# A fused convolution and SwiGLU kernel: the value half takes its feature chunks in turned order, fetches go to 128 partitions, and one queue carries all transfers

## The chip, the cores and the metric

The kernel runs on one core of a Trainium2 chip. The metric is the device time of one execution in microseconds. A profiled execution gives the span from the first to the last instruction of the program and the trace that the lines below come from.

## The reference

Two blocks follow each other. The first is a causal depthwise convolution with 7 taps, softmaxed per head (8 heads of 24 channels), over x of 8 x 4096 x 192. The second is a SwiGLU layer without bias over the resulting 32768 tokens.

```python
w = softmax(weight)                       # 8 heads x 7 taps
x = conv(x_padded, w)                     # (8, 4096, 192) -> (32768, 192)
rms = np.sqrt(np.mean(x * x, axis=-1, keepdims=True) + 1e-06)
xn = x / rms * rms_g
g = xn @ w_gate                           # 192 -> 1536
silu = g * (1.0 / (1.0 + np.exp(-g)))
val = xn @ w_val                          # 192 -> 1536
return (silu * val @ w_out).astype(np.float32)   # 1536 -> 192
```

## The kernel before

**Tiling.** The tokens are taken in 32 "pairs" of 1024 (two groups g of T = 512). The 192 features are three chunks of 64 rows (`KP = 3`, `HP = 64`). Partitions 0 to 63 (`LOW`) compute the gate product and partitions 64 to 127 (`UPP`) the value product, side by side on TensorE; each half needs all three chunks of the tokens, so the normalized tokens stand twice in SBUF, in three slots (k = 0, 1, 2) of the tile `xb` (`rb`). In the kernel before, slot k has chunk k in both halves.

**The way of one pair.** Two pairs ahead of its products, x is loaded to `xh` (L148, eight transfers `ld`, one for each head, runs of 96 bytes; nine in every fourth pair), convolved (`cv`, L442), squared and summed, and scaled by POOL (`mul`, L492). Eight transfers `pl` (`put_away`, L1050) write the heads to a tile `xd` in DRAM, features by tokens. The transfers `ft` (`fetch`, L638) bring `xd` back into `xb`. Then each slot is split in three parts: ACT copies a rounded part (`n`, L667), DVE makes two more (`l` L816, `d` L818); sums of slots 0 and 1 (`x_sum`, L833) are split in the same way. TensorE multiplies the parts with weight pieces (L906), ACT takes silu (L983), DVE multiplies with the value product (L990), and TensorE makes the output product (L933). Transfers `st` (`leave`, L1039) write the result.

**The ring.** The split weights lie in DRAM (`wd`, written by `prepare`, L768). Each pair needs 45 pieces of 192 KB, through a ring of 10 slots in SBUF. `ring_load` (L785) is put on SyncE's queue at the place of the last product that uses a slot, and waits there for TensorE.

**What sets the order.** The order of all work is written out by hand in strings: `FIRST` for the first pair, then `ORDER` for each pair, and `LINE` for TensorE's products. The letter ahead of a word is its engine: A is ACT, V DVE, G POOL, S SyncE; `p3` means three products. Instructions of one engine, transfers included, run in that order, so a transfer that waits holds up what stands behind it on its queue. Hardware semaphores of transfers go round eight lanes over both queues: a transfer waits until the one eight places before it has landed. `queue(eng)` picks ACT's queue for A and SyncE's for S. In the steady part ACT issues the eight `pl`, both halves of slot 0 (`ft.0`, `ft.1`) and five of the ten `st`; SyncE issues the ring loads, `ft.2` to `ft.5`, the `ld` and the other five `st`.

**Pieces in xb.** A row of 1024 tokens is kept as `CUT = 4` pieces of 256, each followed by two unused elements (`GAP = 258`), so that one row of a fetch is four runs of 1 KB. `lent` (in the space of the later ring) has the same form for pair 2.

**Pair 0** has no fetch: `cross` turns it on TensorE and copies it to `xb` in a layout of its own, where the value half already has other chunks than the gate half; `AT` (L1071) says which weight slot belongs to which.

Of the kernel before, what the change touches and what calls it, by code (L numbers as in the profile page):

```python
# [11 lines left out]
F32 = mybir.dt.float32  # L12
F32R = mybir.dt.float32r
AF = mybir.ActivationFunctionType
ALU = mybir.AluOpType
# [5 lines left out]
def kernel(  # L21
# [10 lines left out]
    nc = tc.nc  # L32
    P = nc.NUM_PARTITIONS
# [10 lines left out]
    T = 512  # L44
    PT = 2 * T
    NJ = PT // P
    HALO = K - 1
    HP = P // 2
    KP = D // HP
# [9 lines left out]
    LOW, UPP = slice(0, HP), slice(HP, P)  # L59
# [5 lines left out]


    NP = FC // 2
    CUT = 4
    GAP = PT // CUT + 2
    SPAN = 1509  # L70
    SPLIT = 2.0**-12
    HIGH = 0xFFFFF000
# [2 lines left out]
    ORDER = (  # L75
        "Vd.0 An.4 An.3 Ac2- p5- Gh4.2- Vl.2 Vd.4 Vh4.3- Vl.3 Vd.3 Vl.0 Vd.2 Vh4.0- Vh4.5-",
        "p8- Gh4.4- Gh4.1- VT11- VC22- p2- p1 Gl.4 Acv0+ Af1.0 VT22- VC21- p1- VT21- p3 Vcv1+",
        "p1 Af3.0 Ast1.2- Vcv2+ Vf4.0 p3- p3 Aga.0 Ast1.0- Vcv3+ VT12- Vma.0 Sst0.2- Agc.0",
        "Ast0.3- p1 Vf5.0 p2 Vcv4+ p1 Vmc.0 Vcv5+ p2 Sst1.3- p1 Sst0.4- Sst0.0- Agb.0 Ast1.1-",
        "Agc.1 Ast0.1- Vmb.0 p2 Vcv6+ Agd.0 p2 Aga.1 Vmd.0 Vma.1 Vmc.1 p1 Asq+ Vred+ p1 Af1.2",  # L80
        "Sst1.4- Gh1.0 Agb.1 Vmb.1 p1 Gpow+ p3 Af3.2 p1 Vf4.2 p4 Aga.2 Agd.1 Vma.2 Vbc+ Vf5.2",
        "Gmul+ p1 Agc.2 p1 Apl.0+ Apl.1+ Apl.2+ p1 Vmd.1 Vmc.2 p6 Agd.2 Agb.2 Apl.3+ Vmb.2",
        "Vmd.2 Apl.4+ p1 Agb.3 Aga.3 Apl.5+ p1 Vmb.3 Vma.3 p4 Af1.4 Vf3.4 Agc.3 Apl.6+ Apl.7+",
        "p3 Vmc.3 p1 Vf4.4 p2 Aga.4 Gh1.1 p1 Agd.3 Aft.0+ Sft.2+ Vma.4 Vf5.4 Vh3.1 Sft.3+",
        "Aft.1+ Sld.0++ Vmd.3 Sft.4+ Sld.1++ Sft.5+ Sld.2++ Sld.3++ Sld.4++ Sld.5++ Sld.6++",
        "Sld.7++ p7 Gh1.3 Agc.4 Agd.4 Vmc.4 Vmd.4 Agb.4 p1 Vh1.2 Vh3.0 Vmb.4 p7 An.0+ p1",
        "Aga.5 Agd.5 p1 Vh1.4 An.1+ Vx1+ Vmd.5 Vma.5 p1 Gh3.3 p2 Gh3.2 Agb.5 p2 Gh3.4 p2 Gx3+",
        "Agc.5 Vd.1+ p1 Vh2.0 Vmc.5 Vh2.1 Vmb.5 Vh1.5 Vh2.2 Vh3.5 Vl.1+ Vh2.5 Vh2.4 Ac1 p1",
# [2 lines left out]
    FIRST = (  # L91
        "p1 Vcv5+ W p2 Vcv6+ p1 Aga.0 Vma.0 p2 Asq+ W W p1 Agb.0 W Vmb.0 W p1 Vred+ p2 Agc.0",
        "Vmc.0 W p1 Gpow+ W W W p1 W p1 Agd.0 W Vmd.0 p1 Vbc+ Vh1.0 p1 Gmul+ p1 Aga.1 Vh3.0 W",
        "Vma.1 p1 W W W W p1 W p1 Agb.1 Apl.0+ Vmb.1 p1 Apl.1+ p1 Apl.2+ W p1 Agc.1 Apl.3+ W",
        "W W Vmc.1 Apl.4+ p1 W W Apl.5+ p1 Apl.6+ p1 Agd.1 Apl.7+ Vmd.1 p1 Vh1.1 W p1 W W W",
        "p1 Aga.2 Vh3.1 W Vma.2 W p3 Agb.2 Vmb.2 W p1 W W W p1 W p1 Agc.2 W Vmc.2 p3 Agd.2 W",
        "Vmd.2 p1 W W W Vh1.2 W p1 W p1 Aga.3 Vh3.2 Vma.3 p2 W p1 Agb.3 W W W Vmb.3 p1 W W p1",
        "Aft.0+ p1 Aft.1+ Agc.3 Sft.2+ Vmc.3 p1 Sft.3+ W p1 Sft.4+ W W W Sft.5+ p1 Agd.3 W",
        "Vmd.3 W p1 Vh1.3 p2 Aga.4 Vh3.3 Vma.4 W p1 W W p1 W p1 Agb.4 W Vmb.4 p3 Agc.4 W",
        "Vmc.4 p1 W p2 Agd.4 An.1+ Vmd.4 Sld.0++ p1 Vx1+ Vh1.4 p1 Gx3+ Vd.1+ p1 Aga.5 Vh3.4",  # L100
        "Sld.1++ Vma.5 Vl.1+ p1 Gx2+ p1 An.2+ p1 Agb.5 Gx4+ Vmb.5 p1 Sld.2++ p1 Sld.3++ p1",
        "Agc.5 Vmc.5 p1 Sld.4++ p1 Sld.5++ Agd.5 p1 An.0+ Vmd.5 p1 Sld.6++ Vh2.0 Vh1.5 p2",
        "Gh2.3 Sld.7++ Vh3.5 Vh2.5 p1 Vh2.1 p1 Vh2.4 p1 Ac1 Vh2.2 p2 R p7 As7 p7",
    )
    LINE = (
        "P1.0 P5.0 P6.0 P2.0 Q1.0 P7.0 P3.0 Q2.0 Ac.1 Q4.0 Q3.0 P4.0 Bc.1 Ec.1 Aa.1 Ba.1 Ea.1",
# [8 lines left out]
    cst = ctx.enter_context(tc.tile_pool(name="cst", bufs=1))  # L115
# [13 lines left out]
    def queue(eng):  # L129
        return nc.scalar if eng == "A" else nc.sync  # L130
# [31 lines left out]
    def load(p):  # L162
# [34 lines left out]
        out=ps[6][:, 0 : H * K], lhsT=ones[:], rhs=w_row[:], start=True, stop=True,  # L197
# [4 lines left out]
    rg_sb = cst.tile([P, KP], F32, name="rg_sb")  # L202
    rg = moe_rms_g.rearrange("(c p) -> p c", p=HP)
# [4 lines left out]
    spc = ctx.enter_context(tc.tile_pool(name="spc", bufs=1))  # L208
# [6 lines left out]
    def words(w):  # L215
        return w.bitcast(U32).rearrange("r (n two) -> r n two", two=2)
# [5 lines left out]
    def load_in(u, q):  # L222
        cols = slice(u * NF * P, (u + 1) * NF * P)
        t = big.tile([P, 2, NF, T], F32, name="ht")
        t = t[:].rearrange("p a f t -> p (a f t)")[:, 0 : KP * NF * P * 2].bitcast(U32)
        t = raw["in", u] = t.rearrange("p (k n two) -> p k n two", k=KP, two=2)
        if u == 0:
            hold(t[:, :, 0, 0].bitcast(F32))
        for w, rows in ((moe_w_gate, LOW), (moe_w_val, UPP)):
            for k in range(KP):  # L230
                q.dma_start(out=t[rows, k], in_=words(w)[k * HP : (k + 1) * HP, cols, :])  # L231

    few = 5
    big1 = spc.tile([P, 22, T], F32, name="part1")
    room1 = big1[:].rearrange("p i t -> p (i t)")
    lent = spc.tile([P, KP * CUT * GAP], F32, name="ring")
    early = room1[:, 10 * T + NJ * D : 10 * T + 4 * NJ * D].rearrange("p (i n) -> p i n", i=3)
    kept = [early[:, i].rearrange("p (j d) -> p j d", d=D) for i in range(3)]
    kept = itertools.cycle(kept)
# [5 lines left out]
    tt = work.tile([P, 9, T], F32, name="tt")  # L245
# [3 lines left out]
    def load_out(i):  # L249
# [22 lines left out]
        out=taps[:], in0=w_sb, in1=stat[:].to_broadcast([P, H, K]), op=ALU.subtract  # L272
# [68 lines left out]
        yield  # L341


    rb = cst.tile([P, KP * CUT * GAP], F32, name="xb")
    xb = rb[:, 0 : KP * PT].rearrange("p (k g t) -> p g k t", k=KP, g=2)

    def pieces_in(t):
        t = t[:, 0 : KP * CUT * GAP].rearrange("p (k c t) -> p k c t", k=KP, c=CUT)
        return t[:, :, :, 0 : PT // CUT]

    rb, lent4 = pieces_in(rb), pieces_in(lent)

    def tokens(p):
        return lent4 if p == 2 else rb
    spare = room1[:, 0 : 10 * T]

    def part(at, m, n):
# [276 lines left out]

    def fetch(p, i, eng="S"):

        k, rows = i // 2, (LOW, UPP)[i % 2]
        queue(eng).dma_start(  # L638
            out=tokens(p)[rows, k],
            in_=scr[p][k * HP : (k + 1) * HP, :].rearrange("p (c t) -> p c t", c=CUT),  # L640
        )

    free = [[0, 1, 2, 3], [0, 1, 2, 3]]

# [147 lines left out]
    def split_of(g, i):  # L792

        if not xsplit:
            xsplit.append(spc.tile([P, 8, T], F32, name="part0"))
            xsplit.append(spc.tile([P, 22, T], F32, name="part1"))
        t, at = ((0, 0), (1, 0), (1, 6), (1, 12), (1, 16))[g]
        if g == 4 and i == 0:
            t, at = 0, 6
        return xsplit[t][:, at + i * 2 : at + (i + 1) * 2, :]  # L800

    def cut(t):
        return t.rearrange("p g (c t) -> p (g c) t", t=PT // CUT)

    def operand(g, p):
        if g < KP:
            return tokens(p)[:, g]
        return cut(tt[:, 0:2, :] if g == 3 else tt[:, 2:4, :])

    def split(act, g, eng, p):  # L810
        src, high, low, mix = operand(g, p), *(cut(split_of(g, i)) for i in range(3))
        e = engine.get(eng)
        if act == "n":
            copy(eng, high.bitcast(F32R), src)
        elif act == "l":
            e.tensor_tensor(out=low.bitcast(F32R), in0=src, in1=high, op=ALU.subtract)  # L816
        else:
            nc.vector.scalar_tensor_tensor(  # L818
                out=mix.bitcast(F32R), in0=high, scalar=1.0 + SPLIT, in1=src,
                op0=ALU.mult, op1=ALU.subtract,  # L820
            )

    def x_sum(i, eng, p):
        n = CUT // 2
        a11, a21, a12, a22 = (
            tokens(p)[:, k // 2, k % 2 * n : (k % 2 + 1) * n] for k in range(4)
        )
        s1, s2, s4, s3 = (cut(tt[:, k : k + 1, :]) for k in range(4))
        dst, a, b, op = {
            1: (s1, a21, a22, ALU.add), 3: (s3, a11, a21, ALU.subtract),  # L830
            2: (s2, s1, a11, ALU.subtract), 4: (s4, a12, s2, ALU.subtract),
        }[i]
        engine[eng].tensor_tensor(out=dst, in0=a, in1=b, op=op)  # L833
# [3 lines left out]
    class Pair:  # L837
# [32 lines left out]
        def products(self):  # L870
            if self.p == 1:
                for j, c in PLAIN:
                    g, f = CELL[c]
                    self.open((j, c), False)
                    for k in range(KP):
                        for h in range(2):
                            nc.tensor.matmul(  # L877
                                out=self.both(j, c)[:, h, :], lhsT=wf[HALF[h], k, 2 * j + f, :],
                                rhs=rb[HALF[h], k, g * CUT // 2 : (g + 1) * CUT // 2],
                                start=(k == 0), stop=(k == KP - 1),  # L880
                                skip_group_check=True,
                            )
                        yield
                todo = [w for w in line_of if w[0][0] == "o"]
            else:
                todo = line_of
            for w, i in todo:
                if w[0] == "o":
                    self.step(int(w[1:]), int(i))
                else:  # L890
                    self.product(w, int(i))
                yield
# [175 lines left out]
        else:  # L1068
            {"sq": square, "red": reduce, "pow": factor, "bc": spread, "mul": scale}[act](p)

    AT = (0, 2, 1), (1, 2, 0)  # L1071

    def plain(hts):

# [107 lines left out]
    load_in(1, nc.sync)  # L1182
    conv_first((1, 3, 5, 6), 2)
    nc.sync.dma_start(out=rg_sb[LOW, :], in_=rg)
    nc.sync.dma_start(out=rg_sb[UPP, :], in_=rg)
    load(1)
    load_in(2, nc.sync)
    load_in(3, nc.sync)
# [99 lines left out]
```

## Time and profile before

| | us |
|---|---|
| median of 3 runs | 2496.06 |
| lowest, highest | 2494.13, 2496.62 |
| profiled execution, its own time | 2501.12 |
| its span | 2499.0 |
| granted TensorE clock | 1.00 of full speed |
| DMA, mean over the span | 165 GB/s |
| packets, share of 16 engines, SyncE's queue (q1) | 567088, 57.9% |
| packets, share of 16 engines, ACT's queue (q10) | 172226, 9.8% |

How to read it: PE is TensorE, PEld its weight loads, DVE VectorE, ACT ScalarE, POOL GpSimd, SP SyncE. Names such as "xb<-xd" give output and input by the program's tiles: "xb<-xd" is a fetch, "xd<-xh" a put, "ring<-wd" a ring load. "SPq" and "ACTq" are transfers issued, or waits, by the engine's sequencer. The chain of work that ended last is followed back from the last instruction through whatever released each step. In a list in order of time the columns are start and length in us, then engine, line and names; a bracket gives the engine's idle time just before and what ended it.

### The profile page before, as it was taken

To read this page: it belongs to the slowest core of one execution; us is meant where nothing else is said; L and a number is where in the kernel's file an instruction comes from. 1 tells how busy PE (TensorE), PEld (TensorE's weight loads), DVE (VectorE), ACT (ScalarE), POOL (GpSimd) and SP (SyncE) were. 2 spreads that over 40 slices of the span, in tenths; PEclk is the share of its full clock that TensorE was granted. 3 is DMA by queue.
4 is the path that set the end of the run, shared out by engine and by line. 5 is a ranking of instruction groups with operands and counts; after the bars stand their busy time and mean duration, and the time that the engine had idled before them with its cause. 6 is when DMAs were issued, how large, how long until landed. Compare 5 with 4: busy or idle time off the path is not lost.

```text
span 2499.0 us, 69483 instructions
## 1 busy us (share of the span) xinstructions
PE 2478.2 (99%) x29332; PEld 1917.1 (77%) x29332; DVE 2010.7 (80%) x2492; ACT 922.9 (37%) x1345; POOL 835.9 (33%) x634
## 2 busy tenths in 40 slices
PE   8999999999999999999999999999999999999999
PEld 5547788878778777778877778777787777777777
DVE  8678887888878788878788788888787888788864
ACT  6343333333334333333333333333343333333331
POOL 0542333333333323243323333233323242433331
PEclk9999999999999999999999999999999999999999
DMA  7365667866678767678666777666687666786653
GB/s 150 60 196 160 158 161 182 196 168 163 157 165 191 174 178 158 154 168 195 177 164 151 167 186 180 178 155 156 171 201 169 172 157 159 176 193 173 159 141 82
DMA packets 739624, 412.24 MB, mean 165 GB/s; under 512 B 509810, under 2 KB 737522, under 8 KB 739314
## 3 DMA queue, kind: packets, MB, share of 16 engines
q1 hardware_dynamic: 567088, 353.78, 57.9%
q10 hardware_dynamic: 172226, 54.03, 9.8%
q8 instruction: 231, 3.78, 0.7%
q14 instruction: 79, 0.65, 0.1%
HBM read 349.26 MB, written 58.39 MB: 163 GB/s over the span
## 4 chain that ended last, share of the span: by engine, by line
PE 89%; DMA 5%; DVE 2%; SPq 1%; issue 1%; POOL 1%; ACT 1%; ACTq 0%; DVEq 0%; POOLq 0%
PE ps L906 51%; PE ps L933 35%; DMA xb<-xd 3%; PE ps L877 2%; DVE ht L990 1%; DVE y L442 0%; ACT tt L983 0%; ACTq L1050 0%; DMA ring<-wd 0%; SPq L231 0%; POOL xh L492 0%; DVE ht L1105 0%; SPq L148 0%; DMA hs<-in_moe_w_out_dram 0%; DMA ht<-in_moe_w_gate_dram 0%
## 5 line engine op out<-in xcount | busy, mean ns | idle before, releaser
L906 PE MATMUL ps<-part,ring 64*128 64x512 f32 x12420 | 1446.2, 389 | 1.2 <-DVE ht L990 0.9
L906 PEld LDWEIGHTS ps<-part,ring 64*128 64x128 f32 x12420 | 1180.4, 184 | 246.3 <-issue 18.2
L983 ACT ACTIVATE tt<-ps 128x512 f32<-128x512 f32 x744 | 430.2, 598 | 753.5 <-PE ps L906 572.8
L990 DVE TENSOR_TENSOR ht<-ps,tt 128x512 f32<-128x512 f32 x744 | 494.9, 684 | 190.6 <-ACT tt L983 185.6
L933 PE MATMUL ps<-ht,wo_sb 128*32 128x384 f32 (+2 forms) x7272 | 474.5, 380 | 7.6 <-DVE ht L990 6.5
L933 PE MATMUL ps<-ht,x 128*32 128x256 f32 (+2 forms) x6696 | 441.9, 379 | 0.0
L933 PEld LDWEIGHTS ps<-ht,wo_sb 128*32 128x32 f32 x7272 | 319.7, 110 | 135.0 <-issue 22.3
L960 POOL TENSOR_TENSOR ht<-ht 128x512 f32<-128x512 f32 x183 | 277.0, 1527 | 434.3 <-PE ps L933 380.0
L960 POOL TENSOR_TENSOR hs<-ht 128x512 f32<-128x512 f32 x90 | 116.5, 1295 | 839.2 <-DVE ht L990 837.4
L933 PEld LDWEIGHTS ps<-ht,x 128*32 128x32 f32 x6696 | 302.4, 110 | 90.7
L442 DVE SCALAR_TENSOR_TENSOR y<-xh,tp,y 128x1536 f32<-128x1536 f32 x186 | 339.5, 1825 | 1.3
L977 DVE TENSOR_TENSOR ps<-ps,tt 128x1024 f32<-128x1024 f32 x180 | 221.2, 1229 | 44.0 <-PE ps L906 35.0
L667 ACT COPY ps<-ps 128x384 f32<-128x384 f32 (+1 forms) x121 | 104.1, 860 | 409.5 <-PE ps L906 305.8
L667 ACT COPY tt<-ps 128x384 f32<-128x384 f32 (+1 forms) x122 | 91.0, 746 | 227.0 <-PE ps L933 207.8
L933 PE MATMUL ps<-hs,x 128*32 128x128 f32 (+2 forms) x2232 | 161.0, 379 | 0.0
L667 ACT CAST part<-xb 128x1024 fp32r<-128x1024 f32 x87 | 91.5, 1051 | 110.2 <-DMA xb<-xd 75.1
L933 PEld LDWEIGHTS ps<-hs,x 128*32 128x32 f32 x2232 | 108.8, 110 | 27.8
L960 DVE TENSOR_TENSOR ht<-ht 128x512 f32<-128x512 f32 x189 | 127.3, 686 | 3.4 <-PE ps L933 3.3
L960 DVE TENSOR_TENSOR ht<-hs,ht 128x512 f32<-128x512 f32 x155 | 122.1, 804 | 2.6 <-PE ps L933 1.1
L960 DVE TENSOR_TENSOR hs<-ht 128x512 f32<-128x512 f32 x96 | 116.5, 1213 | 2.1
L818 DVE SCALAR_TENSOR_TENSOR part<-part,xb 128x1024 fp32r<-128x1024 f32 x87 | 105.4, 1212 | 0.0
L816 DVE TENSOR_TENSOR part<-xb,part 128x1024 fp32r<-128x1024 f32 x87 | 105.3, 1210 | 0.0
(132 smaller groups left out, 1383.0 us busy)
## 6 DMA issues: line engine op xcount, KB each, us to landing
ring<-wd SPq DMA_DIRECT2D x1350, 192.0 KB
xb<-xd SPq DMA_DIRECT2D x122, 256.0 KB
xd<-xh ACTq DMA_DIRECT2D x240, 96.0 KB
xh<-in_x_dram SPq DMA_DIRECT2D x192, 105.0 KB
xb<-xd ACTq DMA_DIRECT2D x58, 256.0 KB
out_dram<-o_sb ACTq DMA_DIRECT2D x92, 96.0 KB
wd<-part SPq DMA_DIRECT2D x5, 1152.0 KB
xh<-in_x_dram SPq DMA_DIRECT2D x56, 98.4 KB
```

Of the source, the lines that this page charges most:

```text
L442: nc.vector.scalar_tensor_tensor(out=y, in0=xk, scalar=w, in1=y, op0=ALU.mult, op1=ALU.add)
L667: nc.scalar.copy(out=dst, in_=src)
L816: e.tensor_tensor(out=low.bitcast(F32R), in0=src, in1=high, op=ALU.subtract)
L818: nc.vector.scalar_tensor_tensor(out=mix.bitcast(F32R), in0=high, scalar=1.0 + SPLIT, in1=src, op0=ALU.mult, op1=ALU.subtract,)
L877: nc.tensor.matmul(out=self.both(j, c)[:, h, :], lhsT=wf[HALF[h], k, 2 * j + f, :], rhs=rb[HALF[h], k, g * CUT // 2 : (g + 1) * CUT // 2], ...
L906: nc.tensor.matmul(out=self.both(j, c)[:, h, :], lhsT=left[HALF[h]], rhs=right[HALF[h]], start=(first and q == 0), stop=True, skip_group_c ...
L933: nc.tensor.matmul(out=self.acc(b)[i * Q : (i + 1) * Q, at : at + n], lhsT=left, rhs=cols, start=fresh, stop=True, skip_group_check=True, ...
L960: engine[eng].tensor_tensor(out=dst, in0=a, in1=b, op=op)
L977: nc.vector.tensor_tensor(out=self.both(j, c), in0=self.both(j, "b"), in1=s5, op=ALU.add)
L983: nc.scalar.activation(out=tt[:, t, :], in_=self.both(j, c)[:, 0, :], func=AF.Silu)
L990: nc.vector.tensor_tensor(out=self.hv(j, "abcd".index(c)), in0=self.both(j, c)[:, 1, :], in1=tt[:, t, :], op=ALU.mult,)
```

## The change

The value half takes the chunks in turned order: its slot k has chunk (k + 1) modulo 3, in the weights (`load_in`), the gains (`rg_sb`) and the tokens. Slot 0 over all 128 partitions is then rows 0 to 127 of `xd`, and slot 1 rows 64 to 191; each is one fetch. Slot 2 still takes two (chunk 2 for the gate half, chunk 0 for the value half). Of the six fetch words of a pair, two issue nothing any more (`ft.1`, `ft.3`). The pieces and their gaps go: a row is 1024 tokens without a break. All `pl`, `ft` and `st` of `ORDER` and `FIRST` that were on ACT's queue go to SyncE's, at the same places; in `FIRST` the `ld` move some words back. The instructions of TensorE, DVE and POOL stay the same in number and order, ACT loses its transfers.

```diff
-        "p1 Af3.0 Ast1.2- Vcv2+ Vf4.0 p3- p3 Aga.0 Ast1.0- Vcv3+ VT12- Vma.0 Sst0.2- Agc.0",
+        "p1 Af3.0 Sst1.2- Vcv2+ Vf4.0 p3- p3 Aga.0 Sst1.0- Vcv3+ VT12- Vma.0 Sst0.2- Agc.0",
...
-        "Gmul+ p1 Agc.2 p1 Apl.0+ Apl.1+ Apl.2+ p1 Vmd.1 Vmc.2 p6 Agd.2 Agb.2 Apl.3+ Vmb.2",
+        "Gmul+ p1 Agc.2 p1 Spl.0+ Spl.1+ Spl.2+ p1 Vmd.1 Vmc.2 p6 Agd.2 Agb.2 Spl.3+ Vmb.2",
...
-        "p3 Vmc.3 p1 Vf4.4 p2 Aga.4 Gh1.1 p1 Agd.3 Aft.0+ Sft.2+ Vma.4 Vf5.4 Vh3.1 Sft.3+",
-        "Aft.1+ Sld.0++ Vmd.3 Sft.4+ Sld.1++ Sft.5+ Sld.2++ Sld.3++ Sld.4++ Sld.5++ Sld.6++",
+        "p3 Vmc.3 p1 Vf4.4 p2 Aga.4 Gh1.1 p1 Agd.3 Sft.0+ Sft.2+ Vma.4 Vf5.4 Vh3.1 Sft.3+",
+        "Sft.1+ Sld.0++ Vmd.3 Sft.4+ Sld.1++ Sft.5+ Sld.2++ Sld.3++ Sld.4++ Sld.5++ Sld.6++",
...
-        for w, rows in ((moe_w_gate, LOW), (moe_w_val, UPP)):
+        for w, rows, turn in ((moe_w_gate, LOW, 0), (moe_w_val, UPP, 1)):
             for k in range(KP):
-                q.dma_start(out=t[rows, k], in_=words(w)[k * HP : (k + 1) * HP, cols, :])
+                at = (k + turn) % KP * HP
+                q.dma_start(out=t[rows, k], in_=words(w)[at : at + HP, cols, :])
...
-    rb = cst.tile([P, KP * CUT * GAP], F32, name="xb")
...
+    rb = cst.tile([P, KP, 2, T], F32, name="xb")
...
-        k, rows = i // 2, (LOW, UPP)[i % 2]
-        queue(eng).dma_start(
-            out=tokens(p)[rows, k],
-            in_=scr[p][k * HP : (k + 1) * HP, :].rearrange("p (c t) -> p c t", c=CUT),
-        )
+        k, half = divmod(i, 2)
+        if k < KP - 1:
+            rows, at, n = slice(0, P), k * HP, P
+        else:
+            rows, at, n = HALF[half], (k + half) % KP * HP, HP
+        if half == 0 or k == KP - 1:
+            queue(eng).dma_start(
+                out=tokens(p)[rows, k],
+                in_=scr[p][at : at + n, :].rearrange("p (g t) -> p g t", t=T),
+            )
...
-    AT = (0, 2, 1), (1, 2, 0)
+    AT = (0, 2, 1), (0, 1, 2)
...
-    nc.sync.dma_start(out=rg_sb[UPP, :], in_=rg)
+    nc.sync.dma_start(out=rg_sb[UPP, 0 : KP - 1], in_=rg[:, 1:KP])
+    nc.sync.dma_start(out=rg_sb[UPP, KP - 1 : KP], in_=rg[:, 0:1])
```

## The prediction, made before the changed kernel ran

> **What bounds the kernel now.** I read the page first: busy shares, then the chain.
>
> ```profile
> PE 2478.2 (99%) x29332; PEld 1917.1 (77%) x29332; DVE 2010.7 (80%) x2492; ACT 922.9 (37%) x1345; POOL 835.9 (33%) x634
> ...
> PE 89%; DMA 5%; DVE 2%; SPq 1%; issue 1%; POOL 1%; ACT 1%; ACTq 0%; DVEq 0%; POOLq 0%
> ```
>
> TensorE is the bound, and its work is not changed. What can be won is the rest of the chain, and the 5% of DMA in it (3% "xb<-xd") belongs to the fetches that the change rebuilds. Second view, the whole chain in order of time: it repeats once a pair, and the long L933 block (x304) is a good mark.
>
> ```profile
> 1249.50 24.84 PE ps L933 x304
> ...
> 1314.71 9.47 DMA xb<-xd
> 1324.61 1.09 ACT tt L983 x2
> 1326.46 24.92 PE ps L933 x304
> ...
> 1402.13 24.84 PE ps L933 x304
> ...
> 1449.54 3.00 POOL xh L492
> ...
> 1454.14 2.21 ACTq L1050
> 1458.34 20.18 PE ps L906 x174
> 1478.53 24.84 PE ps L933 x304
> ```
>
> The three intervals between those marks are 76.96, 75.67 and 76.40 us. Over all thirty, from 186.37 to 2466.32, they sum to 2279.95; the undisturbed ones are 75.55 to 75.7, so thirty at 75.6 would be 2268.0. **12.0 us of stall is all that is to be had in the steady part.** It has two kinds, one in each disturbed interval above: a fetch that lands late, and a put that holds ACT.
>
> The fetch kind, in ACT's timeline of that interval and in SP's:
>
> ```profile
> 1313.71 1.23 ACTq L638 DMA_DIRECT2D xb<-xd  x2
> ...
> 1323.65 1.05 ACT L667 CAST part<-xb 128x1024 fp32r<-128x1024 f32 x1 [5.34 <-DMA xb<-xd]
> 1324.61 1.08 ACT L983 ACTIVATE tt<-ps 128x512 f32<-128x512 f32 x2
> ```
>
> ```profile
> 1314.11 1.20 SPq L638 DMA_DIRECT2D xb<-xd  x2
> 1315.42 0.59 SPq L148 DMA_DIRECT2D xh<-in_x_dram  x1
> 1316.06 1.30 SPq L638 DMA_DIRECT2D xb<-xd  x1
> ```
>
> ACT issues slot 0 (two halves) 0.4 us before SP issues slot 1. The packet records show the 1 KB packets of both queues mixed from 1316 on, then mixed with the 96-byte packets of the x loads; slot 0 is complete only after 9.9 us. The cast waits 5.34 us, and the two silus queued behind it on ACT (L983), which free TensorE's banks, are late. In the interval before (start 1173.80) SP was busy until 1239.56, slot 0 went alone at 1238.07, its packets were through by 1243, and nothing stalled. Over all intervals, measured from the block's start: a cast of slot 0 at 71.85 costs nothing, and each 1 us past about 72.8 costs 1 us.
>
> The put kind: ACT issues three puts behind POOL's multiply; usually the third is out 52.5 us after the block's start, here its issue took 2.21 us and ACT with its silus came 0.8 us late. Seven intervals show ACT 0.36 to 0.8 us behind its usual 64.25 at the fetches, 4.2 us together. The other 7.8 of the 12.0 are the fetch kind.
>
> The third view, waits:
>
> ```profile
> SPq L785 <- PE ps L906: 1073.7, 961, 24.0
> ACT tt L983 <- DMA xd<-xh: 80.5, 37, 4.0
> ACT part L667 <- DMA xb<-xd: 75.1, 19, 5.3
> DVE tt L833 <- DMA xb<-xd: 63.9, 29, 3.2
> ```
>
> SP's queue waits 36 us a pair for TensorE to give ring slots back: it has time, but only as much as its next ring load can spare.
>
> **The change, part by part.** *Merged fetches.* Six transfers of 64 partitions and 1 KB pieces become two of 128 and two of 64, in 4 KB rows; bytes are equal. Prices from the packet records: a lone 64-partition fetch moved 100 packets of 1 KB in 0.5 us, 205 GB/s; ring packets (1536 B, 128 partitions) have a median of 65 ns, 23.6 B/ns on an engine; 3072-byte weight rows (64 partitions) 240 ns; 6912-byte x rows (112 partitions) 338 ns. No row shows 4096 bytes on 128 partitions: 173 ns (ring rate) to 320 (weight rows). I take 200 (x rows, nearest in width), so 8 per engine are 1.6 us per merged fetch (1.4 to 2.6).
>
> *Fetches on one queue.* SP reaches them 64.6 us into the interval (ACT: 64.25), having no ring load left that waits. First packets come 1.7 us after an issue, completion some 0.5 after the last. Slot 0 lands at 64.6 + 1.7 + 1.6 + 0.5 = 68.4 (to 69.4), slot 1 at 70.0 (to 72.0). The cast could start at 71.85 anyway, DVE's first sum now starts at 72.8 to 74.8. So 3 us of cover, and all of the fetch kind goes: -7.8 (between 0 and -7.8). What is late next is nothing: the quiet intervals sit on TensorE.
>
> *Puts and five stores leave ACT.* Its silus no longer stand behind POOL's multiply (end at 50.5) or a slow put: -4.2 (0 to -4.2).
>
> *The same on SP.* Per pair SP gets 8 puts (0.54 to 0.63 us each) and 5 stores (0.33 to 0.67) and loses nothing but the place of two fetches: 62 transfers become 75 (with 45 ring loads), about 7 us of issue in 36 us of waiting. What counts is the ring load right behind. From completion marks and first weight load of each piece I get its margin over 30 pairs:
> - Five stores in a row (three before) stand ahead of piece (2,1), margin median 1.36, least 0.25. SP was through with three at 1213.17 and waited until 1214.68 for TensorE; two more are 0.9 to 1.2. Hidden, by 0.3 to 0.6 us.
> - Three puts stand ahead of piece (4,1), margin median 2.98, least 1.86. In the interval from 1173.80 SP issues the ring load before at 50.53 and would reach the puts at 50.9, after POOL's end at 50.5: no wait. Three puts took ACT 1.96 us, so (4,1) goes out at 52.95 where TensorE allowed 51.21: 1.74 late, 1.2 left. In the seven slow intervals the third put takes up to 1.9 more, and the load is up to 0.7 late. Behind it wait the next ring loads, with 1.9 to 4.5 us of margin.
> - The other puts stand ahead of pieces with median margins of 3.5 and more, and cost under 1.5.
> I take +2.0 for seven times 0.3 (0 to +5).
>
> The row for a ring load beside puts: (4,1) landed in a median of 3.09 us while ACT's puts (24 packets of 18 ns per engine each) ran in the other queue. The Trainium skill, DMA: Bandwidth & Descriptors, section on queues, rings and completion order, says that each DMA engine serves its queues in turn, packet by packet; in one queue the load would then have all three puts ahead of it. If all of their 1.3 us came on top, 1.74 + 1.3 is 0.06 over the median margin, and the sum by that rule would be some 2 us higher. I don't add it, since the puts are issued in those same 1.74 us and drain meanwhile.
>
> *One answer each.* Dropping the padded pieces: DVE's L816 takes 1210 ns from padded xb and from tt, ACT's cast 1051 and 1049, matmul L877 (padded) 589, L1087 (plain) 591: nothing, either way under 5 ns. Turned chunks: same matmuls, same order on TensorE. The third gain transfer (rg): 0.4 us of SP ahead of x loads that are on the chain at 21.44: +0.5 (0 to +0.7). First rows: eight puts move between SP's stores of prepared weights, at most 3 us later, where the fetches at 163 have 13 us of room; the x loads moved back are issued from 179.6 to 187.7 and first read at 201: 0.
>
> **Sum** on the profiled execution (2501.12 us, of which 2499.0 is span): -7.8 - 4.2 + 2.0 + 0.5 = -9.5, 2491.6. The median of the runs, 2496.06, is 5.1 lower. If those 5.1 are stalls that only profiling makes, 6.9 of the 12.0 exist without it, and the gain is 6.9 - 2.0 = 4.9 (2491.2); if they are a fixed cost, it is 9.5 (2486.6). I take the middle: **2489.0**, own range 2484 to 2493. A measurement of this kernel can tell about 0.2% (5 us) from no change.
>
> **Rivals.** (1) *No gain.* Slot 0 goes on landing with everything else: 1.5 MB at the 205 GB/s of a lone half are 7.7 us, and 64.6 + 1.7 + 7.7 is 74.0, where the slow intervals are now; what ACT saves goes to the ring margins. 2492 to 2500. For it: DMA engines are full (packet times over 16 engines sum to more than the clock) from 1240 to 1251. Against: the quiet interval, where slot 0 went first. The Trainium skill, same page, section "Issuing engines are not separate DMA queues", has it that all queues share the 16 engines and a second issuer saves only sequencer time; by that rule the move of queues wins nothing. The trace agrees on the mixing, not that order is worthless. Chance 0.2.
>
> (2) *Slower: SP's order starves the ring.* The third put on SP blocks, since ring loads already fill the queue that on ACT was empty. It decides from 1.8 us for that put (0.56 usual, 2.45 seen). At 2.4 in every pair, (4,1) goes out at 54.7, 3.5 late, lands 0.5 to 1.3 after TensorE wants it: 15 to 39 us, less the 12, so 2499 to 2523, middle 2511. For it: SP's fetch behind two x loads blocked for 4.85 us. Against: three puts are 72 packets an engine, and only two ring loads of 8 are in flight. Chance 0.2.
>
> (3) *The rows are slower than any seen*, over 700 ns per 4 KB, so that slot 1 passes 75: no row supports it; inside rival 1's time.
>
> **Numbers.** Forecast 0.6 (0.5 below 2491.1, 0.1 within 0.2%), rival 1 0.2 (within), rival 2 0.2 (nearly all slower). Faster 0.5, same 0.31, slower 0.19. Range 2484 to 2510: it holds the forecast, rival 1, and half of rival 2.
>
> **What would show it.** Right: "DMA xb<-xd" gone from the chain, ACT's L667 and DVE's L833 no longer waiting for it, all marks 75.6 apart, cast of slot 0 at 71.85. Wrong: "PE ps L906" or its weight loads waiting for "DMA ring<-wd" some 57 us into the interval, third puts of over 1.8 us on SP, or casts still at 73 to 74.

## The result, and the profile after

The changed kernel takes **2491.22 us** (median of 20 runs, 2489.73 to 2495.6); the kernel before, beside it, 2496.36 (20 runs, 2492.63 to 2500.95). The ratio is 0.9983, with a 95% interval of 0.9976 to 0.999: faster by 0.17% (the medians alone are 5.1 us, 0.21%, apart), which is just about the 0.2% that the prediction named as the least that can be told from no change. The profiled execution took 2491.27 us, with a span of 2489.5.

The page of the profile after, busy shares and chain by engine:

```profile
PE 2475.4 (99%) x29332; PEld 1971.8 (79%) x29332; DVE 2014.9 (81%) x2492; ACT 926.5 (37%) x1345; POOL 847.1 (34%) x634
...
PE 95%; DMA 2%; DVE 1%; SPq 1%; issue 1%; POOL 0%; ACT 0%; DVEq 0%; POOLq 0%; ACTq 0%
```

PE's share of the chain rose from 89% to 95%, DMA's fell from 5% to 2%, ACT's and its queue's to nothing. The chain in order of time (start and length in us), three marks and what lies ahead of the first; the output block that was L933 is L925 now:

```profile
1235.45 0.42 SPq L637
...
1235.92 9.51 DMA xb<-xd
...
1245.53 0.06 DVE tt L826
...
1246.14 0.70 DVE ht L982
1246.88 24.91 PE ps L925 x304
...
1278.52 44.03 PE ps L898 x382
1322.55 24.84 PE ps L925 x304
...
1354.12 44.04 PE ps L898 x382
1398.16 11.84 PE ps L925 x144
```

From 1246.88 to 1322.55 and on to 1398.16 nothing but TensorE is on the chain: 75.67 and 75.61 us. The lines ahead of the first mark belong to one of the two intervals in which a fetch is still late: the fetch that lands at 1245.43 is that of slot 1, and DVE's sum L826 waits for it. The thirty intervals run from 186.96 to 2456.81, 2269.85 us, where the kernel before needed 2279.95. I call what thirty intervals take above 30 x 75.6 the *excess*: it was 11.9 us and is 1.8, most of it in two intervals (76.39 and 75.94).

Waits, the lines that answer to those of before:

```profile
ACT tt L975 <- PE ps L898: 719.7, 481, 4.8
DVE tt L826 <- DMA xb<-xd: 54.9, 29, 3.5
ACT part L666 <- DMA xb<-xd: 13.6, 4, 3.6
```

```profile
SPq L784 <- PE ps L898: 856.6, 762, 23.8
```

ACT's cast waits for a fetch in 4 intervals in place of 19, and ACT's silu no longer waits for a put (it did for 80.5 us). DVE still waits nearly as long for slot 1. In 28 intervals that costs nothing; in two it is what is left of the stall. SyncE waits 217 us less for TensorE, because it issues thirteen more transfers a pair.

ACT's cast and DVE's timeline in one of these two, the interval from 1171.01:

```profile
1243.36 1.05 ACT L666 CAST part<-xb 128x1024 fp32r<-128x1024 f32 x1 [3.59 <-DMA xb<-xd]
```

```profile
1245.53 0.69 DVE L826 TENSOR_TENSOR tt<-xb 128x512 f32<-128x512 f32 x1 [3.10 <-DMA xb<-xd]
1246.14 1.28 DVE L982 TENSOR_TENSOR ht<-ps,tt 128x512 f32<-128x512 f32 x2
```

The cast starts 72.35 us into the interval, 0.5 us after the harmless 71.85, and that isn't what costs: slot 0 landed as late (72.37) in the interval from 1549.4, which took 75.66 us. DVE's sum of slots 0 and 1 (L826) starts only at 1245.53, behind slot 1, and the product L982, for which TensorE waits, stands behind it. In both slow intervals (slot 1 at 74.95 and 74.50) the interval is 1.44 us longer than slot 1's landing, so that slot 1 begins to cost at about 74.2.

The completion marks say that slot 0 lands at 71.03 (median over the intervals, in us from the interval's start) in place of 72.75, and at most at 72.37 in place of 74.15; slot 1 lands at 73.35 in place of 73.62.

### The profile page after: what moved, and what is told of

It is laid out like the page before. It is cut to its first block, busy times and chain, and to the rows that moved or that the text cites. A ratio compares the mean times of both kernels' runs of the same rounds, so it can differ in the third digit from the quotient of the medians.

```text
span 2489.5 us, 69349 instructions
## 1 busy us (share of the span) xinstructions
PE 2475.4 (99%) x29332; PEld 1971.8 (79%) x29332; DVE 2014.9 (81%) x2492; ACT 926.5 (37%) x1345; POOL 847.1 (34%) x634
## 4 chain that ended last, share of the span: by engine, by line
PE 95%; DMA 2%; DVE 1%; SPq 1%; issue 1%; POOL 0%; ACT 0%; DVEq 0%; POOLq 0%; ACTq 0%
PE ps L898 57%; PE ps L925 36%; PE ps L870 2%; DMA xb<-xd 1%; DVE ht L1097 0%; SPq L146 0%; SPq L230 0%; DVE y L436 0%; DMA hs<-in_moe_w_out_dram 0%; DMA x<-in_x_dram 0%; DMA ht<-in_moe_w_gate_dram 0%; DMA ht<-in_moe_w_val_dram 0%; DVE part L336 0%; POOL part L327 0%; DVE part L321 0%
## 5 line engine op out<-in xcount | busy, mean ns | idle before, releaser
L898 PEld LDWEIGHTS ps<-part,ring 64*128 64x128 f32 x12420 | 1234.7, 184 | 188.1 <-issue 18.3
L982 DVE TENSOR_TENSOR ht<-ps,tt 128x512 f32<-128x512 f32 x744 | 495.8, 685 | 190.0 <-ACT tt L975 184.9
L925 PE MATMUL ps<-ht,wo_sb 128*32 128x384 f32 (+2 forms) x7272 | 474.7, 380 | 1.9 <-DVE ht L982 1.0
L925 PE MATMUL ps<-ht,x 128*32 128x256 f32 (+2 forms) x6696 | 441.9, 379 | 0.0
L925 PEld LDWEIGHTS ps<-ht,wo_sb 128*32 128x32 f32 x7272 | 320.1, 110 | 128.7 <-issue 23.1
L925 PEld LDWEIGHTS ps<-ht,x 128*32 128x32 f32 x6696 | 302.5, 110 | 90.7
L969 DVE TENSOR_TENSOR ps<-ps,tt 128x1024 f32<-128x1024 f32 x180 | 221.3, 1229 | 42.6 <-PE ps L898 35.6
L925 PE MATMUL ps<-hs,x 128*32 128x128 f32 (+2 forms) x2232 | 161.0, 379 | 0.0
L925 PEld LDWEIGHTS ps<-hs,x 128*32 128x32 f32 x2232 | 108.8, 110 | 27.8
L666 ACT CAST part<-xb 128x1024 fp32r<-128x1024 f32 x87 | 91.4, 1050 | 89.5 <-PE ps L898 75.9
L952 DVE TENSOR_TENSOR hs<-ht 128x512 f32<-128x512 f32 x96 | 121.8, 1269 | 2.1
```

The lines of the kernel that those rows point to most:

```text
L666: nc.scalar.copy(out=dst, in_=src)
L898: nc.tensor.matmul(out=self.both(j, c)[:, h, :], lhsT=left[HALF[h]], rhs=right[HALF[h]], start=(first and q == 0), stop=True, skip_group_c ...
L925: nc.tensor.matmul(out=self.acc(b)[i * Q : (i + 1) * Q, at : at + n], lhsT=left, rhs=cols, start=fresh, stop=True, skip_group_check=True, ...
L969: nc.vector.tensor_tensor(out=self.both(j, c), in0=self.both(j, "b"), in1=s5, op=ALU.add)
L982: nc.vector.tensor_tensor(out=self.hv(j, "abcd".index(c)), in0=self.both(j, c)[:, 1, :], in1=tt[:, t, :], op=ALU.mult,)
```

## The experiments

The columns behind the ratio are from one profiled execution each: the excess, the number of intervals above 75.9 us, and when slots 0 and 1 have landed (median, then the latest, of 29: the last interval has no fetch). Each ratio is to the kernel before run beside it on the same chip, whose median was 2495.14 to 2497.2 us in the experiments, so the ratios compare the rows better than the times do. The profiled execution of e2 (2490.43 us) is the fastest of its eleven, that of e9 (2493.55) the slowest of its eleven.

| run | us, median | ratio to before, interval | excess | over 75.9 | slot 0 | slot 1 |
|---|---|---|---|---|---|---|
| before (e0: again) | 2496.36 (2499.44) | 1 | 11.9 (9.6) | 14 (11) | 72.75, 74.15 | 73.62, 74.75 |
| after | 2491.22 | 0.9983 [0.9976, 0.999] | 1.8 | 2 | 71.03, 72.37 | 73.35, 74.95 |
| e1 one queue | 2534.97 | 1.0147 [1.0133, 1.0161] | 42.6 | 29 | 74.03, 76.08 | 72.55, 74.82 |
| e8 one queue, in order | 2491.07 | 0.998 [0.9971, 0.9989] | 0.9 | 1 | 70.90, 72.20 | 73.52, 74.67 |
| e9 two queues, in order | 2492.02 | 0.9983 [0.9974, 0.9992] | 3.7 | 5 | 71.37, 72.78 | 73.22, 74.23 |
| e2 merge alone | 2493.59 | 0.9985 [0.9976, 0.9994] | 1.6 | 2 | 71.22, 73.31 | 72.21, 74.23 |
| e3 after, puts on ACT | 2491.93 | 0.9974 [0.9964, 0.9985] | 1.7 | 2 | 70.54, 72.97 | 72.87, 74.76 |
| e4 unmerged, in order | 2489.72 | 0.9978 [0.997, 0.9987] | 0.1 | 0 | 70.50, 71.94 | 73.12, 74.00 |
| e11 the same again | 2489.14 | 0.997 [0.996, 0.998] | 0.1 | 0 | 70.64, 71.31 | 73.07, 74.03 |
| e10 after again | 2490.94 | 0.9983 [0.9974, 0.9992] | 2.1 | 3 | 70.89, 72.39 | 72.99, 75.02 |
| e7 x loads last | 2492.51 | 0.9989 [0.9981, 0.9998] | 2.1 | 2 | 71.15, 73.13 | 73.51, 75.12 |
| e6 eight puts in a row | 2511.27 | 1.0065 [1.0051, 1.0079] | 21.2 | 21 | 70.94, 73.05 | 73.22, 74.95 |
| e12 before, puts on SyncE | 2583.19 | 1.0351 [1.0334, 1.0368] | 89.9 | 29 | 69.11, 70.08 | 76.88, 78.28 |

One reading holds for the whole table: an execution's time less its excess is between 2488.7 and 2489.9 us in all fourteen. Nearly all that the kernels differ by lies in the thirty intervals.

### Is the kernel before always so disturbed? (e0)

> The kernel before, unchanged, for a second profile. The first profiled execution took 2501.12 us, at the top of the 20 timed runs (2492.63 to 2500.95). If stalls vary from run to run: time 2493 to 2498, and the thirty intervals exceed 75.6 us by about the time less 2489, so 5 to 9 us, and not 12.0, with both kinds (late fetch, slow put) still there. If profiling itself makes the stalls: 2500 or more and some 12 us again.

2499.44 us with an excess of 9.6: a little above what the first reading expects and below what the second does. It lies within the 18 executions of the kernel before on that chip (2493.79 to 2502.16). The disturbance varies from one execution to the next, and the one that the prediction started from was slower than all twenty beside the changed kernel. That profiling slows the kernel isn't seen: the profiled executions of e2 and e4 are the fastest of theirs.

### The parts by themselves (e1, e2, e3)

**e1**: the layout of before, with `ORDER` and `FIRST` of the changed kernel, so that six 64-partition fetches go out on SyncE.

```diff
-"p3 Vmc.3 p1 Vf4.4 p2 Aga.4 Gh1.1 p1 Agd.3 Aft.0+ Sft.2+ Vma.4 Vf5.4 Vh3.1 Sft.3+",
-"Aft.1+ Sld.0++ ...
+"p3 Vmc.3 p1 Vf4.4 p2 Aga.4 Gh1.1 p1 Agd.3 Sft.0+ Sft.2+ Vma.4 Vf5.4 Vh3.1 Sft.3+",
+"Sft.1+ Sld.0++ ...
```

> All transfers on SyncE's queue, but fetches as before: six of 64 partitions, 1 KB pieces, no turned order. Theory A (the order on one queue does it): both halves of slot 0 land first, median 71 to 71.5 us into the interval (before 72.75), excess over 75.6 below 3 us, time 2490.5 to 2492.5. Theory B (the merged 128-partition fetch with long rows does it, the queue is worthless): slot 0 at 72.5 or later, excess 4 to 8 us, time 2494 to 2496. If each does half: 71.5 to 72.3, 2492 to 2494.

1.5% slower, which neither theory had. Waits of e1, then its chain:

```profile
ACT part L667 <- DMA xb<-xd: 122.7, 23, 6.5
...
PE 85%; DMA 7%; SPq 2%; DVE 2%; issue 2%; ACT 1%; POOL 0%; ACTq 0%; DVEq 0%; POOLq 0%
```

The words of the fetches stand in the order 0, 2, 3, 1. On two queues that hurt less; on one queue slot 0's second half, `ft.1`, is fourth of the six and lands at 74.03, 1.2 us past the 72.8 from which a late cast costs. Each of the 29 intervals with a fetch is 2.87 to 2.92 us longer than slot 0's landing, so that every us past 72.7 was paid in full; added up, that is the whole 42.6 us. In the changed kernel `ft.1` issues nothing, so that the order of the words is harmless there.

**e2**: the layout and the merged fetches of the change, with `ORDER` and `FIRST` of before (puts, five stores and slot 0's fetch on ACT).

> Turned order and merged fetches, but the puts, slot 0's fetch and five stores on ACT's queue as before. Theory A (order on one queue): slot 0 on ACT's and slot 1 on SyncE's queue mix packet by packet, slot 0 lands at 72.3 or later, slow puts still hold ACT, excess 5 to 10 us, time 2494 to 2497. Theory B (merging): slot 0 at 71 or earlier, what is left is the put kind alone, excess 2 to 4 us, time 2491 to 2493.

As much as the change within the intervals, 0.9985 against 0.9983: merging alone wins it. Its excess of 1.6 is that of its fastest execution. Both kinds of stall are still there, once each: a slot 0 that lands at 73.31, and an ACT that comes to its fetch at 64.85.

**e3**: the changed kernel with the eight puts of `ORDER` back on ACT.

```diff
-"Gmul+ p1 Agc.2 p1 Spl.0+ Spl.1+ Spl.2+ p1 ...
+"Gmul+ p1 Agc.2 p1 Apl.0+ Apl.1+ Apl.2+ p1 ...
```

> The changed kernel with the eight puts alone back on ACT's queue (steady part). If the put kind is a cause of its own: in the intervals where the third put is slow (over 1.5 us, some 6 of 30) ACT's silus come late and the interval is 0.4 to 0.8 us longer, excess 4 to 6 us (changed kernel 1.9), time 2492.5 to 2495. If it was only the lateness of ACT's own fetches that cost: excess below 2.5, time 2490.5 to 2492.

No slower than the changed kernel. Its excess of 1.7 us sits in two intervals (76.72 and 76.11), and in both the fetch of slot 0 was issued late (65.75 and 65.15).

### The order of the halves or the queue? (e8, e9)

**e8** is e1 with the fetch words of `ORDER` in the order 0, 1, 2, 3, all on SyncE.

> The kernel before (64-partition fetches, 1 KB packets), with all transfers of the steady part on SyncE's queue, as in the experiment on the queue alone, but with the six fetches in the order slot 0, slot 0, slot 1, slot 1, slot 2, slot 2. In that experiment slot 0's second half stood fourth and landed at 74.03 us into the interval; the second place landed at 71.17. Theory A (only the order of the words hurt there; one queue by itself does no harm): slot 0 is complete at about 71.2, slot 1 at about 74.0, the 42.6 us of excess over 75.6 us an interval fall to 2 to 9, and the time is 2491 to 2498. Theory B (putting everything on one queue harms by itself, in a place that the order does not touch): the time stays above 2515. If it is no slower than the merged version (2490 to 2493), the merge is not needed at all, only one queue in the right order.

**e9** is the kernel before with two words of `ORDER` changed, on two queues, with everything else on ACT as it was:

```diff
-"... Agd.3 Aft.0+ Sft.2+ Vma.4 Vf5.4 Vh3.1 Sft.3+",
-"Aft.1+ Sld.0++ ...
+"... Agd.3 Aft.0+ Sft.1+ Vma.4 Vf5.4 Vh3.1 Sft.3+",
+"Aft.2+ Sld.0++ ...
```

> The kernel before in everything (64-partition fetches with 1 KB packets, two queues, puts and stores on ACT), but that in the steady part the two queues take one half of slot 0 each, and behind it one half of slot 1 each (before, ACT's queue had both halves of slot 0 and SyncE's both of slot 1, so that slot 1's first half went ahead of slot 0's second). Theory A (the order in which the halves are served is all that cost time; the second queue does no harm): slot 0 is complete at 71.0 to 72.0 in place of 72.4 to 72.75, the excess falls from 10 to 12 us to 1 to 4, 2490 to 2494. Theory B (two queues mix their packets, or ACT's fetch behind ACT's other work is late, and that costs in any order): slot 0 stays at 72.4 and later, 2494 to 2498.

Theory A in both. e8 and e1 differ in the order of the fetch words and by 42 us of excess. e9 keeps two queues, 1 KB packets and 64 partitions, and slot 0 is never later than 72.78. Waits of e8, then of e9, then e9's chain in one of its disturbed intervals (from 717.15):

```profile
DVE tt L833 <- DMA xb<-xd: 63.6, 29, 3.3
ACT part L667 <- DMA xb<-xd: 6.4, 2, 3.3
```

```profile
DVE tt L833 <- DMA xb<-xd: 55.1, 29, 2.9
ACT part L667 <- DMA xb<-xd: 6.6, 2, 3.3
```

```profile
770.39 4.89 DMA ring<-wd
775.30 0.54 ACTq L1050
775.94 1.01 ACT ps L667
776.99 16.61 PE ps L906 x144
```

What is left in e9 is the other kind of stall, now alone: a put that ACT issues late, with work behind it that frees TensorE's banks. Six intervals have it, 0.88, 0.78, 0.69, 0.34, 0.32 and 0.25 us, 3.3 us together; in each ACT comes to its fetch later than 64.45. With the puts on SyncE (e8) 0.9 us is left in all, 0.5 of it in one interval in which slot 1 landed at 74.67. The first line of the chain tells why the put shown is late: it waits for the ring load that had its completion semaphore before it, and goes out 0.02 us after that has landed.

Such waits aren't rare. In the undisturbed intervals, too, puts go out 0.02 us after a ring load has landed; there the sixth put starts by 56.43, and in four of the six disturbed ones it starts at 56.7 or later (58.15 in this one). In two of the six a put also took 1.96 and 2.06 us to issue in place of 0.6.

### Packet length and 128 partitions (e4, e10, e11)

**e4** and **e11** are one kernel: the changed kernel with each 4 KB row fetched in 64-partition halves, in slot order, on SyncE. **e10** is the changed kernel on the chip of e11.

```diff
-        if k < KP - 1:
-            rows, at, n = slice(0, P), k * HP, P
-        else:
-            rows, at, n = HALF[half], (k + half) % KP * HP, HP
-        if half == 0 or k == KP - 1:
-            queue(eng).dma_start(out=tokens(p)[rows, k], ...
+        at = (k + half) % KP * HP
+        queue(eng).dma_start(out=tokens(p)[HALF[half], k], ...
```

> The changed kernel with its fetches not merged: six transfers of 64 partitions with 4 KB rows, in slot order on SyncE's queue. It stands between the run with 1 KB packets in slot order and the changed kernel. Theory A (128 partitions in one transfer are what makes the fetch quick): landings as with 1 KB packets in slot order, slot 0 at about 71.2 and slot 1 at about 74, excess 2 to 9, 2491 to 2498. Theory B (rows of 4 KB in place of 1 KB pieces are): landings as in the changed kernel, 71.0 and 73.35, excess 1 to 3, 2490 to 2493. If both are equal to the changed kernel, neither matters by itself.

> The changed kernel again, for comparison with the unmerged 4 KB halves on the same chip. Both theories: 2490 to 2492, excess of 1 to 3 us.

> The version with unmerged halves of 4 KB rows in slot order on one queue again, beside the changed kernel. Theory A (halves in order land slot 0 some 0.5 us earlier than one 128-partition fetch, and hardly any interval is disturbed): 2489.0 to 2490.5, 1 to 2 us under the changed kernel. Theory B (its 2489.7 was the chip): equal to the changed kernel within 0.5 us.

The halves are the fastest of all the versions: 2489.14 us (9 runs, 2488.42 to 2489.95) beside 2490.94 of the changed kernel (11 runs, 2489.57 to 2494.79), so it beats both kernels. For e4's question the answer is that neither theory holds: 1 KB pieces or 4 KB rows, 64 or 128 partitions, slot 0 lands between 70.5 and 71.03. The merged fetch has the longer tail: slot 1 at most at 75.02 (e10), with the halves at 74.03, short of the 74.2 from which it costs. The three slow intervals of e10 (75.93, 76.19 and 76.46) are those in which slot 1 landed later than 74.5, 1.37 to 1.44 us before their end. e11's chain has only TensorE in it between marks:

```profile
1169.52 24.84 PE ps L921 x304
...
1245.13 24.84 PE ps L921 x304
...
1320.74 24.84 PE ps L921 x304
```

75.61 and 75.61 us, with 0.1 us of excess over thirty: nothing is left to win in the steady part without less work for TensorE.

### What stands behind the fetches (e7)

**e7**: both fetches of slot 2 ahead of all x loads.

```diff
-"Sft.1+ Sld.0++ Vmd.3 Sft.4+ Sld.1++ Sft.5+ Sld.2++ ...
+"Sft.1+ Vmd.3 Sft.4+ Sft.5+ Sld.0++ Sld.1++ Sld.2++ ...
```

> The changed kernel with both fetches of slot 2 ahead of all eight x loads, which stood two behind one and three behind the other. Slot 2 landed at 75.4 and 77.3 us into the interval and kept DVE waiting 55 us in all. Theory A (TensorE is at its floor, DVE's wait has cover): excess stays at 1 to 2.5 us, 2489 to 2494, no difference from the changed kernel. Theory B (the late sums of slot 2 set the one or two slow intervals): excess under 1 and 1 to 3 us faster than the changed kernel. If x loads were what slows the fetches of slots 0 and 1, these land earlier too, by over 0.3 us.

No gain: slot 2 is complete at 75.30 in place of 77.33, slots 0 and 1 no earlier, and the excess is 2.1. The x loads between the fetches don't delay slots 0 and 1, and slot 2 had cover.

### The price of SyncE's order (e6)

**e6**: the changed kernel with five more puts behind the first three.

```diff
-"Gmul+ p1 Agc.2 p1 Spl.0+ Spl.1+ Spl.2+ p1 ... Spl.3+ ... Spl.4+ ... Spl.5+ ... Spl.6+ Spl.7+",
+"Gmul+ p1 Agc.2 p1 Spl.0+ Spl.1+ Spl.2+ Spl.3+ Spl.4+ Spl.5+ Spl.6+ Spl.7+ p1 ...
```

> The changed kernel with all eight puts in a row on SyncE, right behind POOL's multiply (three there before). SyncE reaches them at 50.9 us into the interval; at 0.62 us each they end at 55.9 in place of 52.8. The ring load behind them (the first of four) had a margin of 3.46 us (median, least 2.01) in the changed kernel, the second 3.38, the third 3.06 (least 1.04); 3.1, 3.1 and 2.7 us go off these. Theory A (the ring's order on SyncE is a real limit, my second rival's mechanism, only further away than I put it): margins of -0.5 to 0.5, TensorE's L898 waits for the ring in many pairs, 0.3 to 1 us each, 2500 to 2520; if further puts block at 1.2 us and more, over 2540. Theory B (the slack of the ring covers it): no ring wait, within 0.2% of the changed kernel, 2488 to 2496.

Theory A, 2511.27. SyncE's timeline in one interval (start 1181.16), then TensorE's waits:

```profile
1231.99 5.25 SPq L1042 DMA_DIRECT2D xd<-xh  x8
1237.34 8.45 SPq L784 DMA_DIRECT2D ring<-wd  x12
```

```profile
PE ps L898 <- DMA ring<-wd: 10.9, 22, 1.4
```

```profile
PEld ps L898 <- DMA ring<-wd: 12.1, 28, 1.2
```

The three ring loads behind the puts have median margins of 0.10, 0.17 and 0.04 us, where the changed kernel had 3.46, 3.38 and 3.06. The waits of matmuls and weight loads, 10.9 and 12.1 us, account for the excess of 21.2. A delay of some 3 us on SyncE, as long as the margins read from completion marks, is about where it begins to cost.

### The puts alone, on the kernel before (e12)

**e12**: the kernel before, with puts and stores on SyncE, and slot 0's halves left on ACT (`FIRST` is that of the changed kernel).

> The kernel before with the eight puts and the five stores on SyncE's queue, as the change has them, and the fetches as before (slot 0's halves on ACT, 1 KB packets). My prediction put 4.2 of 12.0 us to the puts that hold ACT; by that, theory A: 2491 to 2493, an excess of 5 to 8 in the profile. Theory B (the order of the fetches is the whole cause; a late ACT only mattered as it made slot 0 later): no difference from before, 2494 to 2498, an excess of 8 to 12, casts of slot 0 still waiting in some 19 intervals.

3.5% slower: it answers another question than the one it was made for. SyncE's timeline in the interval from 1209.23, ACT's, and SyncE's waits:

```profile
1269.79 9.84 SPq L785 DMA_DIRECT2D ring<-wd  x6
1279.68 1.24 SPq L638 DMA_DIRECT2D xb<-xd  x2
```

```profile
1273.49 1.19 ACTq L638 DMA_DIRECT2D xb<-xd  x2
```

```profile
SPq L785 <- DMA xb<-xd: 194.6, 61, 6.5
```

Six ring loads take 9.84 us. The third, issued at 1277.21, carries the completion semaphore of ACT's first fetch, which landed at 1277.15; the fourth, at 1278.36, that of ACT's second, landed at 1278.30. SyncE is held 6 us in each pair for transfers it has nothing to do with: slot 1's fetches go out at 70.5 in place of 64.6 and land at 76.9, and ring loads come late as well. Slot 0, alone on the engines, lands at 69.1, the earliest of all, and that is of no use. Whether the puts on SyncE would help the kernel before without this wait wasn't seen; the nearest to it is e8 against e9 (2491.07 and 2492.02), where all transfers move to SyncE with slot 0 in order.

## Why the prediction was right, and where it was not

**The bound.** That the excess of 12.0 us is all there is to win held: time less excess is the same within 1.2 us in fourteen executions.

**The fetch kind, -7.8.** The size fits the one execution that it was read from: with its stall gone and the put kind still there (e9), 8.3 of 11.9 us are gone. By the medians of one chip (2495.98 and 2492.02) the order alone is worth 4.0. Of the mechanism, it was right that slot 0 has to go first, and more so than the text knew: e8 and e9 each win it by order alone, without a merge; the queue by itself, in the order of the words, costs 38 us (e1). What helps is that nothing of slot 1 is issued ahead of slot 0's second half. The threshold of 72.8 held: slot 0 is later in 13 intervals of before, 29 of e1 and in none of the changed kernel.

The landing times of that step were mis-sized: 68.4 and 70.0 were forecast, 71.03 and 73.35 measured. The packets of 4096 bytes took a median of 159 ns (the estimate was 200), but the mean is 236, and the last packets of a transfer come one by one while the engines' summed packet time falls to between 0.5 and 0.1 of the clock (1243.5 to 1245.5 in the interval above). Of the 3 us of cover, 0.8 was left, for slot 0 to 71.85 and for slot 1 to the 74.2 from which it costs. So "what is late next is nothing" is right in 28 intervals; in two slot 1's tail (74.95 and 74.50) made them 76.39 and 75.94. Why the last packets trickle stays open.

**The put kind, -4.2.** Right in kind: 3.3 us in e9 and about 1.6 in e3, with the puts on ACT; 4.2 was on the high side. Its cause was half seen. The prediction saw a slow issue, and in four of its seven intervals a put did take 2.01 to 2.45 us. The other three have no slow issue; in them, as in e9, puts wait for ring loads through common semaphores.

**The ring, +2.0.** Nothing was paid: no TensorE wait for the ring is left on the page. The step had the wrong piece. (4,1) doesn't stand right behind the three puts; (4,4) does, issued at 52.83 in the interval from 1171.01, with a margin of 4.29 before and 3.46 after (least 2.01). (4,1) is two loads further back and waits for TensorE until 54.5, as before. Five stores ahead of (2,1) were hidden, as forecast (median margin 1.36, then 1.39).

(4,4), right behind the three puts of its own queue, landed 2.62 us after its issue; before, with the puts in the other queue, it took 3.53. The Trainium skill (DMA: Bandwidth & Descriptors, "Queues, rings and completion order") says that each DMA engine serves its queues in turn, packet by packet. The delay of up to 1.3 us that the prediction drew from this rule is shown by no run.

**The start, +0.5.** Measured 0.6: the first mark moved from 186.37 to 186.96.

**The sum.** On the profiled executions, 2491.6 forecast and 2491.27 measured. That this is so close is partly luck, since terms made up for each other: +2.0 too much for the ring, 1.8 us that were left of the stalls. The median, 2489.0, is 2.2 us too low. The step that failed is the middle between two readings of 5.1 us. The first reading, that the 5.1 are stalls and not a fixed cost, gives 2491.2, and is what happened, though they were those of a slow execution and not of profiling: medians less the 2489.3 of undisturbed work leave stalls of 7.1 us before and 1.9 after, a gain of 5.1.

**The rivals.** Rival 1 (slot 0 goes on landing at 74.0) didn't happen; its time range began at 2492, 0.8 us above the result. On one queue it does happen if the order is wrong (e1, 2534.97), and then at a far higher price than the 2492 to 2500 it was given. With slot 0 in order, one queue and two are alike, 0.998 (e8) and 0.9983 (e9). The Trainium skill (same page, "Issuing engines are not separate DMA queues") says that a second issuer saves sequencer time alone; these two runs agree. But by e12 two issuers can cost 87 us, through the semaphores that they share. Rival 2 (SyncE's order starves the ring) has a real mechanism, shown by e6, with a price inside the 15 to 39 us it was given; its point was wrong: the third put took 1.75 us at most (a second one 2.06), and the margin behind it allowed 3.

## What to carry to other kernels

When several transfers feed one consumer, look at the place of the last one that it needs, and at what is served ahead of it; here the order of the fetch words was worth 42 us, and the shape of the transfers 2. Read margins (completion mark to first use) piece by piece along the queue, and make sure by issue times which piece stands behind the inserted work. Before work moves between queues, list which transfers share a completion semaphore across them: a wait for a stranger's transfer shows in the profile as a ring load waiting for a fetch.

## What the runs showed of the hardware that was not expected

- A 128-partition transfer with 4096-byte packets ended no earlier than the two 64-partition halves issued in order: slot 0 at 70.9 (e10) and at 70.64 (e11), although the median packet took 159 ns in the one and 268 ns in the other. It had the longer tail, and the version with halves was 1.8 us faster.
- Shared completion semaphores cost up to 87 us in e12 (against the kernel before on the same chip), and in e9 they are what holds ACT's puts in at least four of its six disturbed intervals, 2.0 of 3.3 us.
- Some puts took 1.6 to 2.45 us to issue in place of 0.6 (six in the kernel before, four in e9). In the kernel before all six began within 0.4 us of a packet of 16384 bytes on queue q8 (kind "instruction", 231 in the execution). There, 214 puts of the steady part began with no such packet near, and none of these took over 0.82 us; in the changed kernel nine of the 17 with one near took over 1.2 us, and none of the other 215. That the packet is what holds them is not shown.
